# Early tiles of the busiest expert: their products issued in counted portions around the last chunk's routing, with weight splits, loads and output moved behind that chain

## The chip, the cores and the metric

One core of a Trainium2 chip runs the kernel. The metric is the device time of one execution in microseconds (us), the lower the better. TensorE is called PE here, VectorE DVE, ScalarE ACT, GpSimd POOL and the queue of SyncE SP, as in the profile.

## The reference

Three parts follow each other, all in float32.

```python
# 1: attention, 4 batches x 8 heads x 576 positions x 64: a local band plus a 4x downsampled one
x = (out_up + out_local)              # laid out as 2304 tokens x 512
# 2: a dense layer pair, 512 -> 2048 -> 512
h = np.maximum(x @ w_in, 0.0)
x = h * h @ w_out
# 3: eight experts, each token goes to one
logits = x @ w_gate                   # 2304 x 8
e_idx = np.argmax(logits, axis=1)
gate_w = softmax(logits)[token, e_idx]
eom = 1.0 / (1.0 + np.exp(-(x @ w_output_gate)))
for e in range(8):
    mask = e_idx == e
    ye = np.maximum(x[mask] @ w1[e], 0.0) @ w2[e]      # 512 -> 1024 -> 512
    out[mask] = gate_w[mask, None] * eom[mask, e, None] * ye
```

## The kernel before

**Stages.** Attention makes the 512 x 2304 activations in tiles of [128, 576]. Part 2 goes over nine chunks of 256 tokens: `l1` (products named `ph`) and `l2` (named `y`). Each float32 operand is split into a high and a low part, and each product is three passes (`PASSES`: high by high, high by low, low by high). When a chunk's `y` is done, `finish_y` copies it out of PSUM as `yr` (one half by ACT, one by DVE), and `routing` decides where its rows go.

**Routing of a chunk** is a generator with steps parted by `yield`. First it transposes `yr` (`yt`, L536) and copies the result out (`yT`). Then it makes logits (`lg`, L544), copies them (`lgt`) and sums their four parts (`lg` again, L550). DVE copies the sums (`lgs`, L553) and finds each row's expert. Then PE counts the rows of each expert ahead of each row (`rk`, L579), DVE makes the row's place (`di`, L588), and two indirect DMAs on POOL's queue put the token numbers into two lists in DRAM (`orders`, L594). The rows themselves go to a table in DRAM (`ytab`, L600).

**Part 3** takes one expert after the other in tiles of 128 rows. A tile's rows are gathered from `ytab` by the numbers in the lists, transposed (`px`), split (`xs`, high by ACT and low by DVE), multiplied by `w1` (`ph`, `layer1`), transposed again (`pt`, split into `hs`) and multiplied by `w2` (`py`, `layer2`). Weights come in eight loads of 128 x 1024 for each expert (0 to 3 are `w1`, 4 to 7 are `w2`); each is split by ACT (high) and DVE (low) out of a staging buffer. There are three such buffers at first, so load i waits for the DVE half of split i-3.

**The seam between parts 2 and 3.** No list is complete before the last chunk is routed. To have work for PE there, the kernel takes the expert with most rows so far (`choose`, "lead") and computes two of its tiles early, during the last chunk: `lead_1` makes `phf` (24 products a tile), `lead_turn` transposes (`ptf`) and splits (`hsf`), `lead_2` makes `pyf` (24 products) and puts the result out. `feed(n)` splits the first n of 16 weight pieces named in `LINE`. After the last routing, the heads of the lists are read back (`c4`, L943) and DVE makes the row numbers of the first two tiles of expert 0 (`cf`, `cd`, `ci`), which POOL gathers. The whole lists are read as `og` and transposed on PE (`po`, L986); DVE makes the index table of all later gathers from that.

**What sets the order.** The kernel is traced in program order, and a scheduler then orders each engine's instructions by its own simulated time. `high_priority` lets a block go first where it can; `issue_after(x)` queues a block's instructions behind x, but only those on the engine of x, and without waiting for x to finish. Each engine then runs its instructions strictly in that order.

```python
    route(1)
    lead_1(0, 0)
    feed(12)
    route(1)
    lead_1(0, 1)
    route(8)
```

Of the kernel before, what the change touches and what calls it, by code (L numbers as in the profile page):

```python
# [25 lines left out]
def attn_moe_kernel(  # L26
# [503 lines left out]
    def routing(c):  # L530
# [3 lines left out]
        for i in range(2):  # L534
            for kk in range(KC):
                nc.tensor.transpose(out=pt[:, i, P * kk:P * kk + P],  # L536
                                    in_=yr[:, i, P * kk:P * kk + P], identity=ident)
        yT = cv.tile([P, 2, DM], F32, tag="raw", name=f"yT{c}")
        nc.scalar.activation(out=yT[:, 0, :], in_=pt[:, 0, :], func=AF.Copy)
        nc.scalar.activation(out=yT[:, 1, :], in_=pt[:, 1, :], func=AF.Copy)  # L540
        yield
        pl = psa.tile([P, 2, DM], F32, tag="at", name=f"lg{c}")
        for kk in range(KC):
            nc.tensor.matmul(pl[32 * kk:32 * kk + 32, 1, 0:CH], lhsT=wg[:, kk, :],  # L544
                             rhs=yT[:, :, P * kk:P * kk + P], start=True, stop=True)
        lt = cv.tile([P, DM], F32, tag="tmp", name=f"lgt{c}", bufs=TMPB)[:, 0:CH]
        nc.scalar.activation(out=lt, in_=pl[:, 1, 0:CH], func=AF.Copy)
        plv = pl[:, 0, 0:4 * E].rearrange("p (i e) -> p i e", i=2)
        for i in range(2):
            nc.tensor.matmul(plv[:, i, :], lhsT=lt[:, P * i:P * i + P], rhs=psum4,  # L550
                             start=True, stop=True)
# [26 lines left out]
        for i in range(2):  # L578
            nc.tensor.matmul(prv[:, i, :], lhsT=sut, rhs=oh[:, i, :], start=True, stop=False)  # L579
            nc.tensor.matmul(prv[:, i, :], lhsT=ones, rhs=seen, start=False, stop=True)  # L580
# [12 lines left out]
        for i in range(2):  # L593
            nc.gpsimd.indirect_dma_start(  # L594
# [115 lines left out]
    def lead_split():  # L710
# [10 lines left out]
        most["hr"] = [late.tile([P, F2], F32, tag="hr", name="hr")] * 2  # L721

    def lead_1(x, h):

        ph = (psh.tile([P, DM], F32, tag="ph", name=f"phf{x}_{h}") if x == 0 else
              psy.tile([P, DM], F32, tag=f"y{h}", name=f"phf{x}_{h}"))
        half_layer1(ws[-1, 0], most["xs"][:, x], ph, most["hr"][x], h)

    def lead_turn(x):
# [3 lines left out]
        for h in range(2):  # L733
            t = psh.tile([P, DM], F32, tag="ph", name=f"ptf{x}_{h}")
            for c in range(4):
                f0 = 512 * h + P * c
                nc.tensor.transpose(out=t[:, P * c:P * c + P], in_=most["hr"][x][:, f0:f0 + P],
                                    identity=ident)
            nc.scalar.activation(out=hs[2 * h], in_=t, func=AF.Copy)
            nc.vector.tensor_sub(out=hs[2 * h + 1], in0=t, in1=hs[2 * h].bitcast(F32))  # L740
        most["hs", x] = hs

    def lead_2(x):
        py = psy.tile([P, DM], F32, tag=f"y{x}", name=f"pyf{x}")
        hs = most["hs", x]
        for kf in range(KF):
            for n, (a, b) in enumerate(PASSES):
                o = P * (kf % 4)
                nc.tensor.matmul(py, lhsT=hs[2 * (kf // 4) + a][:, o:o + P], rhs=ws[-1, 1](b, kf),
                                 start=(kf == 0 and n == 0), stop=(kf == KF - 1 and n == 2))  # L750
# [5 lines left out]
        nc.gpsimd.indirect_dma_start(  # L756
            out=out, out_offset=bass.IndirectOffsetOnAxis(ap=oi[:, 0:1], axis=0), in_=ob,
            in_offset=None, bounds_check=NT - 1, oob_is_err=False)
# [22 lines left out]
    def half_layer1(w1v, xs, ph, hr, h):  # L781
        for n in range(3 * KC):
            kk, (a, b) = n // 3, PASSES[n % 3]
            nc.tensor.matmul(ph, lhsT=xs[:, a, P * kk:P * kk + P],  # L784
                             rhs=w1v(b, kk)[:, 512 * h:512 * h + 512],
                             start=(n == 0), stop=(n == 3 * KC - 1))
        nc.scalar.activation(out=hr[:, 512 * h:512 * h + 512], in_=ph, func=AF.Relu)  # L787

    def layer1(w1v, xs, ph, hr):
        for h in range(2):  # L790
            half_layer1(w1v, xs, ph[h], hr, h)
# [139 lines left out]
    route(1)  # L931
    lead_1(0, 0)
    feed(12)
    route(1)
    lead_1(0, 1)
# [4 lines left out]
    with tc.high_priority():  # L940
        c4 = const.tile([P, 2, 2 * FT], F32, name="c4")
        for i, o in enumerate(orders):
            nc.sync.dma_start(out=c4[:, i, :], in_=lists(o)[0, :, 0:2 * FT])  # L943
# [252 lines left out]
```

## Time and profile before

| | |
|---|---|
| time, median of 3 runs | 917.65 us (916.43 to 921.03) |
| the profiled execution | 917.83 us |
| its span, first to last instruction | 916.0 us |
| PE busy | 823.5 us (90%) |
| DVE, ACT, POOL busy | 451.5, 395.9, 341.3 us |
| mean granted TensorE clock | 0.967 of full |
| DMA | 103.45 MB, mean 113 GB/s |

The span is what lies between the core's first and last instruction; the time holds 1.8 us around it. PE is busy almost everywhere; the page's 40 slices show two places where it is not, the start, and slices 28 and 29 of 40, which are the seam.

### The profile page before, as it was taken

The numbers are of one execution on the slowest core, as the hardware profiler recorded it, in microseconds if no ns is written. First come the engines' busy times: TensorE is split into PE (matmuls) and PEld (weight loads), VectorE is DVE, ScalarE is ACT, GpSimd is POOL, SyncE is SP. The second block draws the span as 40 slices with busy tenths as digits, with TensorE's granted clock in tenths as the row PEclk, the third lists the DMA queues.
The fourth block names the chain that finished last, engine by engine and source line by source line (L and its number), as shares of the span: only waits on it lengthen the run. The fifth ranks groups of instructions, "written<-read, shape, count | busy, mean of one in ns | idle before, by whom it ended". The sixth has DMA issues, their size and how long they took to land. (4 is left out here: it accounts for less than half of the span.)

```text
span 916.0 us, 15844 instructions
## 1 busy us (share of the span) xinstructions
PE 823.5 (90%) x5983; PEld 697.6 (76%) x5983; DVE 451.5 (49%) x960; ACT 395.9 (43%) x900; POOL 341.3 (37%) x411
## 2 busy tenths in 40 slices
PE   4588979987999989999999999993699989999996
PEld 3377869876888878888989898772587767878785
DVE  7987685777365554343222225425443556434111
ACT  3634555554443443343333335542544656434221
POOL 4556554544345543543333233313231232312111
PEclk9988989998899999999999999996799999999999
DMA  9851221454034332110000024415854594531101
GB/s 324 255 160 46 99 95 69 167 178 161 24 100 78 78 101 78 28 29 25 1 24 1 24 70 138 140 46 180 297 197 132 202 335 140 207 133 35 50 34 35
DMA packets 35519, 103.45 MB, mean 113 GB/s; under 512 B 6836, under 2 KB 6864, under 8 KB 35408
## 3 DMA queue, kind: packets, MB, share of 16 engines
q1 hardware_dynamic: 30000, 87.16, 28.9%
q0 software_dynamic: 5408, 14.88, 5.2%
q8 instruction: 61, 1.00, 0.5%
q14 instruction: 50, 0.41, 0.1%
HBM read 88.16 MB, written 14.65 MB: 112 GB/s over the span
## 5 line engine op out<-in xcount | busy, mean ns | idle before, releaser
L461 PE MATMUL ph<-xc,win 128*128 128x256 f32 x1728 | 244.1, 288 | 14.0 <-DVE g L466 12.1
L461 PEld LDWEIGHTS ph<-xc,win 128*128 128x128 f32 x1728 | 230.0, 193 | 33.1 <-DVE g L466 14.7
L484 PE MATMUL y<-wout,gs 128*128 128x512 f32 x864 | 231.8, 400 | 4.8 <-ACT gs L469 3.7
L470 POOL TENSOR_TENSOR gs<-g,gs 128x256 fp32r<-128x256 f32 x144 | 111.8, 779 | 201.6 <-ACT gs L469 129.7
L484 PEld LDWEIGHTS y<-wout,gs 128*128 128x128 f32 x864 | 151.7, 189 | 34.4 <-ACT gs L469 4.5
L466 DVE SCALAR_TENSOR_TENSOR g<-ph,g 128x256 f32<-128x256 f32 x144 | 60.2, 420 | 172.8 <-ACT g L465 172.6
L465 ACT ACTIVATE g<-ph 128x256 f32<-128x256 f32 x144 | 54.7, 382 | 122.6 <-PE ph L461 105.1
L469 ACT ACTIVATE gs<-g 128x256 fp32r<-128x256 f32 x144 | 59.6, 415 | 60.2 <-DVE g L466 54.8
L784 PE MATMUL ph<-we_wa,xs 128*128 128x512 f32 x228 | 64.5, 419 | 13.0 <-PEq L1127 8.4
L1024 POOL DMA_INDIRECT xg<-ytab,apt x23 | 32.2, 1400 | 84.4 <-ACT apt L787 44.4
L784 PEld LDWEIGHTS ph<-we_wa,xs 128*128 128x128 f32 x228 | 42.8, 197 | 24.9 <-ACT we_wd L650 8.8
L784 PE MATMUL ph<-we_wb,xs 128*128 128x512 f32 x228 | 61.4, 406 | 0.0
L1064 DVE COPY g<-g 128x2 f32<-128x2 f32 x19 | 3.2, 169 | 103.8 <-ACT ob L1055 103.8
L1051 PE MATMUL py<-we_wc,hs 128*128 128x512 f32 x216 | 54.1, 399 | 0.0
L1051 PE MATMUL py<-we_wd,hs 128*128 128x512 f32 x216 | 53.3, 396 | 0.0
L784 PEld LDWEIGHTS ph<-we_wb,xs 128*128 128x128 f32 x228 | 44.6, 196 | 11.1
L1055 ACT ACTIVATE ob<-py,g 128x512 f32<-128x512 f32 x18 | 12.4, 687 | 88.3 <-PE py L1051 78.5
L1058 POOL DMA_INDIRECT out_dram<-ob,oi x18 | 18.6, 1033 | 82.6 <-issue 34.6
L1051 PEld LDWEIGHTS py<-we_wd,hs 128*128 128x128 f32 x216 | 40.6, 188 | 9.8
L1051 PEld LDWEIGHTS py<-we_wc,hs 128*128 128x128 f32 x216 | 39.7, 188 | 8.7
L787 ACT ACTIVATE apt<-ph 128x512 f32<-128x512 f32 x38 | 22.8, 600 | 49.3 <-PE ph L784 49.2
L448 DVE TENSOR_TENSOR xc<-xT,xc 128x256 fp32r<-128x256 f32 (+3 forms) x76 | 37.3, 540 | 2.8 <-ACT xc L447 2.8
(257 smaller groups left out, 1223.3 us busy)
## 6 DMA issues: line engine op xcount, KB each, us to landing
apt<-in_w_dram SPq DMA_DIRECT2D x37, 512.0 KB, 4.1
stg<-in_w_dram SPq DMA_DIRECT2D x35, 512.0 KB, 7.2
apt<-in_qk_dram SPq DMA_DIRECT2D x10, 576.0 KB, 4.9
raw<-in_w_out_dram SPq DMA_DIRECT2D x11, 512.0 KB
raw<-in_w_in_dram SPq DMA_DIRECT2D x11, 512.0 KB, 3.3
ytab<-yr SPq DMA_DIRECT2D x18, 260.0 KB, 2.3
yr<-ypart SPq DMA_DIRECT2D x8, 512.0 KB, 4.3
sparewb<-in_qk_dram SPq DMA_DIRECT2D x6, 576.0 KB, 13.8
```

Source lines behind the costliest of these rows:

```text
L448: nc.vector.tensor_sub(out=t[:, 1, hp, done:done + ln], in0=src, in1=hi.bitcast(F32))
L461: nc.tensor.matmul(ph, lhsT=wv[:, wh, kk, :], rhs=x[:, xh, kk, :], start=(n == 0), stop=(n == 3 * KC - 1))
L465: nc.scalar.activation(out=g, in_=ph, func=AF.Relu)
L466: nc.vector.scalar_tensor_tensor(out=g, in0=ph, scalar=0.0, in1=g, op0=ALU.max, op1=ALU.mult)
L469: nc.scalar.activation(out=gs[:, 0, :], in_=g, func=AF.Copy)
L470: nc.gpsimd.tensor_sub(out=gs[:, 1, :], in0=g, in1=gs[:, 0, :].bitcast(F32))
L484: nc.tensor.matmul(yps[c][i], lhsT=gs[:, gh, P * i:P * i + P], rhs=woutv[f // FQ][:, f % FQ, wh, :], start=(first and n == 0), stop=(last ...
L784: nc.tensor.matmul(ph, lhsT=xs[:, a, P * kk:P * kk + P], rhs=w1v(b, kk)[:, 512 * h:512 * h + 512], start=(n == 0), stop=(n == 3 * KC - 1))
L787: nc.scalar.activation(out=hr[:, 512 * h:512 * h + 512], in_=ph, func=AF.Relu)
L1024: nc.gpsimd.indirect_dma_start(out=xg[:], out_offset=None, in_=ytab[:], in_offset=bass.IndirectOffsetOnAxis(ap=idx, axis=0))
L1051: nc.tensor.matmul(py, lhsT=hs[:, a, P * kf:P * kf + P], rhs=w2v(b, kf), start=(kf == 0 and n == 0), stop=(kf == KF - 1 and n == 2))
L1058: nc.gpsimd.indirect_dma_start(out=out, out_offset=bass.IndirectOffsetOnAxis(ap=oi[:, 0:1], axis=0), in_=ob[:], in_offset=None, bounds_che ...
```

## The change

The products of the early tiles become a generator that yields after each product (`lead_1` and `lead_turn` become parts of it). Of them, 10, 4 and 9 are issued behind the named steps of the last routing on PE (`yt`, first `lg`, second `lg`), 39 behind `rk`, and the rest later. The second `yT` copy of the last chunk goes to DVE. `feed` has split 14 pieces, not 12, before the routing, in another order of `LINE`; the two others stand behind `di` on DVE and behind `lgt` on ACT. The early tiles' output is put behind the list's puts on POOL, the loads of expert 1 behind the read of the list heads on SP, and the transposes of the lists behind the last early product on PE. At expert 0, the split of the second tile stands behind that of the first and behind its products, and so do the splits of expert 1's weights behind the first tile's split.

```diff
+        if c < NCH - 1:
+            nc.scalar.activation(out=yT[:, 1, :], in_=pt[:, 1, :], func=AF.Copy)
+        else:
+            nc.vector.tensor_copy(yT[:, 1, :], pt[:, 1, :])
...
-        nc.gpsimd.indirect_dma_start(
-            out=out, out_offset=bass.IndirectOffsetOnAxis(ap=oi[:, 0:1], axis=0), in_=ob,
-            in_offset=None, bounds_check=NT - 1, oob_is_err=False)
+        with tc.issue_after(most["put"].ins):
+            nc.gpsimd.indirect_dma_start(
+                out=out, out_offset=bass.IndirectOffsetOnAxis(ap=oi[:, 0:1], axis=0), in_=ob,
+                in_offset=None, bounds_check=NT - 1, oob_is_err=False)
...
-    LINE += [(lead, i) for i in range(4, 8)] + [(experts[0], i) for i in range(4, 8)]
+    LINE += [(x, i) for j in (4, 6) for x in (lead, experts[0]) for i in (j, j + 1)]
...
-    route(1)
-    lead_1(0, 0)
-    feed(12)
-    route(1)
-    lead_1(0, 1)
+    for _ in lead_1(0):
+        pass
+    feed(14)
+    fill = [lead_2(0), lead_2(1)]
+    for part, n in (("yt", 10), ("lg", 4), ("ps", 9)):
+        route(1)
+        with tc.issue_after(most[part]):
+            drive(fill, n)
     route(8)
...
-    lead_turn(0)
-    lead_1(1, 0)
-    lead_1(1, 1)
-    lead_2(0)
-    with tc.issue_after(most["routed"]):
+    with tc.issue_after(most["rk"]):
+        drive(fill, 39)
+    with tc.issue_after(most["routed"]), tc.issue_after(most["lt"]):
         feed(16)
...
-    lead_turn(1)
-    lead_2(1)
+    with tc.issue_after(most["rk"]):
+        drive(fill, 99)
...
-    with tc.issue_after(most["routed"]):
+    with tc.issue_after(most["routed"]), tc.issue_after(got.ins):
         for i in range(3):
             experts[1].load(i, stages[i])
...
+            with tc.issue_after(most["end"]):
+                nc.tensor.matmul(po[:, 0, h * E * NTL // 2:(h + 1) * E * NTL // 2],
...
+        with ExitStack() as behind:
+            if e == 0:
+                for x in (*first_xs, first_mm):
+                    behind.enter_context(tc.issue_after(x))
+            split_rows(xgs[1 + 2 * (e % 2)], xs1, g1, f"{e}_1")
```

The built order differs from that of before only from the last chunk's end to the first tile of expert 0. On PE, in the last chunk's routing, before: `yt` are the transposes of the chunk's result, `phf` and `ptf` the early tiles' products and transposes, `lg` the logits.

```order
L536 MATMUL yt_6514<-ident,yr_6505 128x128 x4
L784 MATMUL phf_0_6639<-we-1_wa,xsf 128x512 x6
L784 MATMUL phf_0_6639<-we-1_wb,xsf 128x512 x4
L536 MATMUL yt_6514<-ident,yr_6505 128x128 x4
L784 MATMUL phf_0_6639<-we-1_wb,xsf 128x512 x2
L784 MATMUL phf_1_6653<-we-1_wa,xsf 128x512 x3
L737 MATMUL ptf_1_6632<-ident,apt 128x128 x4
L784 MATMUL phf_1_6653<-we-1_wa,xsf 128x512 x3
L784 MATMUL phf_1_6653<-we-1_wb,xsf 128x512 x6
L544 MATMUL lg_6546<-yT_6523,wg 32x256 x4
```

The same place on PE in the change (its line numbers are 3 to 18 higher):

```order
L536 MATMUL yt_6553<-ident,yr_6505 128x128 x8
L745 MATMUL ptf_0_6569<-ident,apt 128x128 x4
L794 MATMUL phf_0_6583<-we-1_wa,xsf 128x512 x2
L745 MATMUL ptf_1_6576<-ident,apt 128x128 x4
L547 MATMUL lg_6586<-yT_6562,wg 32x256 x4
L794 MATMUL phf_0_6583<-we-1_wa,xsf 128x512 x4
L556 MATMUL lg_6586<-psum_82,lgt_6591 128x16 x2
L794 MATMUL phf_0_6583<-we-1_wb,xsf 128x512 x6
L794 MATMUL phf_1_6626<-we-1_wa,xsf 128x512 x3
L585 LDWEIGHTS sut
L585 MATMUL rk_6630<-oh_6609,sut 128x8
```

Before, 24 `phf` products and 4 `ptf` transposes stand between the first `yt` and the first `lg`, and 21 `pyf` products between the first and the second `lg`; now two products and four, and nine before `rk`.

On DVE, at the arithmetic on the list heads, before (`we` are low halves of weight splits, `cf`, `cd`, `ci` the row numbers of the first two tiles):

```order
L651 TENSOR_TENSOR we_wd<-apt,we_wd 128x1024
L651 TENSOR_TENSOR we_wa<-apt,we_wa 128x1024
L945 TENSOR_TENSOR cf<-c_6610 128x4
L947 TENSOR_TENSOR cd<-cf 128x2
L651 TENSOR_TENSOR we_wa<-apt,we_wa 128x1024
L949 SCALAR_TENSOR_TENSOR ci<-cd,star,cf 128x2
```

And in the change:

```order
L595 CAST di_6641<-rsc_6603 128x2
L658 TENSOR_TENSOR we_wd<-apt,we_wd 128x1024 x2
L963 TENSOR_TENSOR cf<-c_6651 128x4
L965 TENSOR_TENSOR cd<-cf 128x2
L967 SCALAR_TENSOR_TENSOR ci<-cd,star,cf 128x2
L672 COPY cntc<-pcc 128x8
L986 CAST nti<-cntc 128x8
L987 TENSOR_SCALAR nti<-nti 128x8
L749 TENSOR_TENSOR hsf_1_6704<-ptf_0_6707,hsf_0_6703 128x512
```

The splits of expert 1 (`we_wa`) are gone from between these rows, and the low part `hsf` of the second early tile, which stood ahead of `di` before, now stands behind `cf`.

On DVE, at the first tiles of expert 0, before (`g` is a copy of two columns of gathered rows, `g_6814` of those of the second tile; `xs_6812` is the first tile's low part):

```order
L1039 COPY g_139<-apt 128x2
L1064 COPY g_6816<-g_139 128x2
L1039 COPY g_6814<-apt 128x2
L1040 TENSOR_TENSOR xs_6812<-px_0_6818,xs_6812 128x512
L1040 TENSOR_TENSOR xs_6806<-px_1_6885,xs_6806 128x512
L651 TENSOR_TENSOR we_wb<-stg_6813,we_wb 128x1024
```

And in the change, where the second `g_139` is that of expert 1's first tile:

```order
L1057 TENSOR_TENSOR xs_6812<-px_0_6818,xs_6812 128x512
L1056 COPY g_6814<-apt 128x2
L658 TENSOR_TENSOR we_wa<-apt,we_wa 128x1024
L1056 COPY g_139<-apt 128x2
L658 TENSOR_TENSOR we_wa<-apt,we_wa 128x1024
L658 TENSOR_TENSOR we_wb<-apt,we_wb 128x1024
L658 TENSOR_TENSOR we_wb<-stg_6813,we_wb 128x1024
L1057 TENSOR_TENSOR xs_6806<-px_1_6885,xs_6806 128x512
```

The first tile's low part no longer stands behind the copy from the second tile's rows; three of expert 1's split halves now stand behind the copy from a gather of expert 1.

## Rows read from the trace of the kernel before

**Rows 1.** Windows of 5 us: length, busy time (instructions) of PE, PEld, DVE, ACT, POOL, clock, DMA share, GB/s.

```profile
625.00:630.00 5.00, 0.00 (x0) 0.00 (x0) 1.23 (x1) 1.12 (x2) 1.51 (x3) 0.65 0.23 30
```

**Rows 2.** Waits after 660 us: who waited for whom, us in all, times, longest.

```profile
PE ph L784 <- PEq L1127: 8.4, 2, 4.4
```

**Rows 3.** Timeline of the last routing: start, length, engine, line, output<-inputs, [idle before <-releaser].

```profile
600.76 0.69 DVE L523 COPY yr<-y 128x512 f32<-128x512 f32 x1 [3.36 <-PE y L484]
...
604.93 0.60 PE L536 MATMUL yt<-ident,yr 128*128 128x128 f32 x4
...
606.06 0.59 ACT L540 ACTIVATE yT<-yt 128x512 f32<-128x512 f32 x1
...
609.17 0.64 PE L544 MATMUL lg<-yT,wg 128*32 128x256 f32 x8
...
612.65 2.26 PE L749 MATMUL pyf<-we-1_wd,hsf 128*128 128x512 f32 x9
614.75 0.51 PE L550 MATMUL lg<-psum,lgt 128*128 128x16 f32 x4
...
615.37 0.19 DVE L553 COPY lgs<-lg 128x32 f32<-128x32 f32 x1 [6.87 <-PE lg L550]
...
619.37 0.16 DVE L588 CAST di<-rsc 128x2 int32<-128x2 f32 x1
```

**Rows 4.** Timeline: list puts and read-backs, of the routing before (570s) and the last.

```profile
571.15 1.07 POOL L594 DMA_INDIRECT order<-row,di  x1 [0.72 <-PE ph L461]
...
575.71 1.95 SPq L699 DMA_DIRECT2D of<-order  x2
...
579.42 0.16 DVE L702 TENSOR_TENSOR oif<-of 128x2 int32<-128x2 f32 x1 [1.30 <-DMA of<-order]
...
619.81 1.69 POOL L594 DMA_INDIRECT order<-row,di  x1 [1.63 <-DVE di L588]
621.81 2.10 POOL L594 DMA_INDIRECT order<-row,di  x1 [0.30 <-issue]
628.80 0.55 POOL L965 DMA_DIRECT2D og<-order  x1 [0.58 <-DMA order<-row,di]
629.29 0.46 SPq L943 DMA_DIRECT2D c<-order  x1
635.82 0.16 DVE L945 TENSOR_TENSOR cf<-c 128x4 f32<-128x4 f32 x1
```

**Rows 5.** Timeline from the last early products to expert 1's first product.

```profile
619.44 1.22 DVE L651 TENSOR_TENSOR we_wc<-apt,we_wc 128x1024 fp32r<-128x1024 f32 x1
...
621.13 2.97 PE L749 MATMUL pyf<-we-1_wd,hsf 128*128 128x512 f32 x12
...
637.54 0.30 DVE L996 CAST apt<-po 128x144 int32<-128x144 f32 x1
...
640.05 0.23 DVE L1002 TENSOR_TENSOR apt<-po,sh 128x64 int32<-128x64 f32 x1
...
645.61 0.17 DVE L1039 COPY g<-apt 128x2 f32<-128x2 f32 x1 [4.00 <-DMA apt<-ytab,ci]
...
646.40 3.76 PE L784 MATMUL ph<-we_wa,xs 128*128 128x512 f32 x8
...
653.86 0.60 PE L1069 MATMUL pt<-ident,apt 128*128 128x128 f32 x4
...
660.19 2.15 PE L784 MATMUL ph<-we_wa,xs 128*128 128x512 f32 x5 [4.38 <-PEq L1127]
```

**Rows 6.** Windows of 0.5 us of PE: length, busy time (instructions), clock, DMA share, GB/s.

```profile
626.00:626.50 0.50, 0.00 (x0) 0.95 0.00 0
...
660.50:661.00 0.50, 0.50 (x3) 0.59 0.87 107
...
663.50:664.00 0.50, 0.50 (x3) 0.50 1.01 352
```

**Rows 7.** DMA issues of 600 to 665 us: queue, count, KB each, median us to landing.

```profile
apt<-ytab,apt POOLq DMA_INDIRECT x3, 6.7
```

More of the change, by code (lines that the diff above doesn't have):

```diff
@@ L579, in routing @@
             nc.tensor.matmul(prv[:, i, :], lhsT=sut, rhs=oh[:, i, :], start=True, stop=False)
-            nc.tensor.matmul(prv[:, i, :], lhsT=ones, rhs=seen, start=False, stop=True)
+            most["rk"] = nc.tensor.matmul(prv[:, i, :], lhsT=ones, rhs=seen, start=False,
+                                          stop=True).ins
             nc.vector.tensor_add(out=seen, in0=seen, in1=oh[:, i, :])
@@ L593, in routing @@
         for i in range(2):
-            nc.gpsimd.indirect_dma_start(
+            most["put"] = nc.gpsimd.indirect_dma_start(
                 out=orders[i][:], out_offset=bass.IndirectOffsetOnAxis(ap=di[:, i:i + 1], axis=0),
@@ L720, in lead_split, with lead_1, lead_2 @@
         most["xs"] = xs
[L721 to L729, printed above, removed]
+        most["hr"] = late.tile([P, F2], F32, tag="hr", name="hr")
+    def lead_1(x):
+        for h in range(2):
+            ph = (psh.tile([P, DM], F32, tag="ph", name=f"phf{x}_{h}") if x == 0 else
+                  psy.tile([P, DM], F32, tag=f"y{h}", name=f"phf{x}_{h}"))
+            yield from half_layer1(ws[-1, 0], most["xs"][:, x], ph, most["hr"], h)
+    def lead_2(x):
         hs = [xp.tile([P, S], F32, tag="xT", name=f"hsf{x}_{i}").bitcast(F32R)[:, 0:512]
@@ L736, in lead_turn @@
                 f0 = 512 * h + P * c
-                nc.tensor.transpose(out=t[:, P * c:P * c + P], in_=most["hr"][x][:, f0:f0 + P],
+                nc.tensor.transpose(out=t[:, P * c:P * c + P], in_=most["hr"][:, f0:f0 + P],
                                     identity=ident)
+                yield
             nc.scalar.activation(out=hs[2 * h], in_=t, func=AF.Copy)
             nc.vector.tensor_sub(out=hs[2 * h + 1], in0=t, in1=hs[2 * h].bitcast(F32))
-        most["hs", x] = hs
-    def lead_2(x):
+        if x == 0:
+            yield from lead_1(1)
         py = psy.tile([P, DM], F32, tag=f"y{x}", name=f"pyf{x}")
-        hs = most["hs", x]
         for kf in range(KF):
@@ L748, in lead_2 @@
                 o = P * (kf % 4)
-                nc.tensor.matmul(py, lhsT=hs[2 * (kf // 4) + a][:, o:o + P], rhs=ws[-1, 1](b, kf),
-                                 start=(kf == 0 and n == 0), stop=(kf == KF - 1 and n == 2))
+                most["end"] = nc.tensor.matmul(
+                    py, lhsT=hs[2 * (kf // 4) + a][:, o:o + P], rhs=ws[-1, 1](b, kf),
+                    start=(kf == 0 and n == 0), stop=(kf == KF - 1 and n == 2)).ins
+                yield
         ob = most["xe"][:, x, 0:DM]
@@ L942, in attn_moe_kernel @@
         for i, o in enumerate(orders):
-            nc.sync.dma_start(out=c4[:, i, :], in_=lists(o)[0, :, 0:2 * FT])
+            got = nc.sync.dma_start(out=c4[:, i, :], in_=lists(o)[0, :, 0:2 * FT])
         cf = const.tile([P, 2 * FT], F32, name="cf")
@@ L1018, in attn_moe_kernel @@
     early[3] = mp2.tile([P, 1024], F32, tag="stg3", name="stg3", bufs=1)
-    hr = most["hr"][0]
+    hr = most["hr"]
     g1, gn, gp = (mp2.tile([P, 2], F32, tag=f"g{i}", name=f"g{i}", bufs=1) for i in range(3))
@@ L1039, in split_rows @@
             nc.vector.tensor_copy(g, xg[:, DM:DM + 2])
-        nc.vector.tensor_sub(out=xs[:, 1, :], in0=px, in1=xs[:, 0, :].bitcast(F32))
+        lo = nc.vector.tensor_sub(out=xs[:, 1, :], in0=px, in1=xs[:, 0, :].bitcast(F32))
+        return hi.ins, lo.ins
     def layer1_here(w1v, xs, name):
-        layer1(w1v, xs, [ps4.tile([P, 512], F32, tag="ph", name=f"ph{name}_{h}")
+        return layer1(w1v, xs, [ps4.tile([P, 512], F32, tag="ph", name=f"ph{name}_{h}")
                          for h in range(2)], hr)
@@ L1097, in attn_moe_kernel @@
             after.place(0)
-            for i in range(4):
-                after.split(i)
+            with ExitStack() as behind:
+                if e == 0:
+                    for x in first_xs:
+                        behind.enter_context(tc.issue_after(x))
+                for i in range(4):
+                    after.split(i)
             for i in range(4, 8):
@@ L1105, in attn_moe_kernel @@
             after.place(1)
-        split_rows(xgs[1 + 2 * (e % 2)], xs1, g1, f"{e}_1")
+        with ExitStack() as behind:
+            if e == 0:
+                for x in (*first_xs, first_mm):
+                    behind.enter_context(tc.issue_after(x))
+            split_rows(xgs[1 + 2 * (e % 2)], xs1, g1, f"{e}_1")
         gather(xgs[2], index(e, 2))
@@ L1109, in attn_moe_kernel @@
             gather(xgs[3 - 2 * (e % 2)], index(e + 1, 1))
-        hand_over(g0, n)
+        turned = hand_over(g0, n)
         if more:
-            split_rows(xgs[0], xs0, g0, f"{e + 1}_0")
+            with tc.issue_after(turned):
+                split_rows(xgs[0], xs0, g0, f"{e + 1}_0")
             if e + 2 < E:
```

46 lines of the change are left out of this document (26 added, 20 removed).

## The prediction

> **What bounds the kernel now.** I read first the windows of 5 us over the page's weak slices, then the timeline of each engine there, then the waits of what follows. The windows show where PE has nothing to do: from 625 to 630 us it is not busy at all and its granted clock falls [rows 1]. The timeline gives the edges: the last early product ends at 624.1 (621.13 + 2.97), and the first product of expert 0 starts at 646.40 [rows 5]. Between them lie only the transposes of the lists and of two tiles of rows: 22.3 us in which PE waits for one chain, and that chain began before 600 us.
>
> The chain is the last routing. The chunk's result is out of PSUM at 601.45 (600.76 + 0.69), its first logits start at 609.17, the second at 614.75, DVE copies them at 615.37 and has the places at 619.37 [rows 3]. Up to the logits' copy that is 13.9 us for little work: the second half of the transposes starts only at 604.93, the first logits stand behind the second tile's products, and the second logits behind 21 products, of which nine are the row from 612.65 to 614.75 [rows 3]. These nine also give the pitch used below: 2.10 / 9 = 0.233 us a product. Then come two list puts, whose landing frees the read-backs at about 628.8 and 629.29, DVE's `cf` at 635.82 [rows 4], and the rows' gathers. At the end the first tile's low part stands on DVE behind a copy that waits for the second tile's gather until 645.61 [rows 5].
>
> What follows the seam takes a gain on: after 660 us PE's largest wait is the branch at L1127, twice, 8.4 us together, 4.4 at most [rows 2]. From expert 1's first product at 660.19 [rows 5] on, PE is the bound, and it has the same work in the same order. So I work out when that product comes. Everything ahead of 600 us keeps its order but for the load order, treated at the end of the next part.
>
> **The change, step by step.** Times are those of the profiled execution, 917.83 us with a span of 916.0, 0.18 above the median of the runs shown.
>
> *Routing on PE and ACT.* One more early product stands ahead of the chunk's last six: the result is out at 601.45 + 0.23 = 601.7. Eight transposes at the pitch of the row (four in 0.60 with their drain [rows 3]) end at 602.8. ACT has a relu copy of the same size ahead and copies its half (0.59 [rows 3]) until 603.45; in the built program DVE's half waits for ACT's, so moving it gains nothing: 0.69 like the copy of the result, to 604.2. The first logits start at 604.25 instead of 609.17. They take 0.64, their copy (half the columns of the 0.59, estimated 0.4) ends at 605.35; the four early products behind them (0.93) hold PE until 605.65, so the second logits start there, and DVE's copy 0.62 later (615.37 - 614.75) at 606.3, 9.1 us earlier than now.
>
> *To the places.* Before, 4.0 us from that copy to `di` (619.37 - 615.37), with two `hsf` parts of some 0.69 in between that now come later. Against that, ACT does two weight halves ahead of the exponentials that DVE waits for, and nine products (2.1) stand ahead of `rk`. Bounds 2.6 and 4.0; by the list of instructions I get 3.9, nearer the upper: `di` at 610.2.
>
> *Puts and read-back.* The first put starts 0.44 after `di` (619.81 - 619.37), the second 2.0 later as in the last routing, where DVE's split halves of 1.22 ran beside it [rows 4, 5], and where they run again: 612.6. If it were as short as in the routing before (1.07 + 0.30), 612.0. From the second put's start to its landing took 7.0 (621.81 to 628.80), with weight loads beside it; in the routing before, a first put took 4.6 (571.15 to 575.71) [rows 4]. The weight loads are now in earlier. So the second read-back is issued between 616.6 and 619.7. It then takes 0.46 to issue and 1.76 to land (577.66, the end of the issue, to 579.42 [rows 4]): the list heads are in SBUF between 618.8 and 621.9. I take the middle, 620.3. No row shows more than an upper end for that read beside weight loads: `cf` ran 6.5 us after its issue, at 635.82, behind a split half [rows 4]. That is the bound on the late side, 626.1.
>
> *The new wait.* DVE now runs `cf` ahead of the second tile's low part `hsf`, so DVE sits from about 612.6 until the heads land. Behind it stand six small operations (0.16 each and the gap, 0.2) and that `hsf` (0.69): it ends at 622.3. PE has by then run nine products to 610.9, 24 to 616.5, eight transposes to 617.5, waited 0.6 for ACT's part, and done two products to 618.6. The third needs `hsf`: PE stalls 3.7 us. That is part of the old stall, come back in the middle of the fill. 22 products are left, 5.1 us: 627.4.
>
> *The clock.* After the last early product PE idled 2.3 us before the clock fell at about 626.45; after the idle of 4.38 it fell at 660.6, once work had begun again, and stood at half until 664.0 [rows 5, 6]. The new stall of 3.7, almost all idle, lies between. I take the fall, as after the 4.38: 3.4 us at half speed cost 1.7, so the products end at 629.1. The Trainium skill speaks against the change in the same sense: TensorE: Matmul & The Clock Gate, section "HAM oscillation — how this bites in real kernels", has waits for data in the midst of matmuls lead to a restart at the lower clock. By it the sum is the one below; were the stall too short for it, 1.7 less.
>
> *First tile of expert 0.* The transposes of the lists, estimated as twice the row of four at 653.86 (0.60 [rows 5]), end at 630.3. DVE's arithmetic took 637.54 to 640.28 with one split half in between: 1.5 without it [rows 5], so 632.0 with semaphores. The low part follows at once (0.69 and a copy): 632.8. By then PE has done the rows' transposes and the four products that need only the high part. The other 20 end at 637.5. The gather of the rows (POOL, from 621) and the transposes' input (the list reads, from about 617) are hidden under the fill. Moving `xs` away from the second gather removes the wait that ended at 645.61 [rows 5].
>
> *To expert 1.* From the end of these products to the branch's end took 6.3 (653.86 to 660.19 [rows 5]); that gives 643.8. DVE gives another date: expert 1's first gather goes out when the arithmetic is done, 632.1, and takes 6.7 [rows 7]: 638.8. Behind its copy DVE now has three split halves (3 x 1.22) and four parts of 0.69, 6.5 in all: 645.3; two products can start ahead of the last: 644.8. The two dates lie close; I take 644.6. Against 660.19 that is 15.6 us. Arithmetic queued behind `po`, the early output behind the puts on POOL, and loads of expert 1 behind the read of the heads on SP cost nothing here: PE is filling, and the loads have from 620 to 630. Without that cover the output put would cost its own 1 us of POOL ahead of the gather.
>
> *Load order.* `LINE` now loads two pieces of expert 0 ahead of two of the lead. ACT's last square of the chunk stands behind the lead's fourth such piece. Its buffer is freed by a DVE half that now stands ahead of the chunk's last two squares on DVE, where before it stood behind them, so I price it at nothing; if the load held ACT, the whole chain would start later by as much.
>
> **Sum:** 917.83 - 15.6 = 902.2, or 902 for the median.
>
> **The rivals.**
>
> *Late reads and gathers.* The heads land between 622 and 626.1, or the gather of expert 1 takes over 7 us under the five loads issued beside it, or the load order holds ACT: each us beyond the estimate costs one. With the heads at 626.1: 902.2 + 5.8 = 908. For it: the old read-backs and gathers all ran beside loads. Against: the earlier loads are done.
>
> *No stall in the fill.* If the heads land before about 616.6, `hsf` is there when PE wants it; neither 3.7 nor 1.7 is paid: 896.8. Against it: a put took 4.6 at least [rows 4], and this asks for 4 from the first put's start to both read-backs in. The Trainium skill's page DMA: Bandwidth & Descriptors, "Anatomy of one DMA — SWDGE (gpsimd) path", puts a transfer at about 2 us plus its bytes; by that estimate the heads would be in at about 616.7, and the sum near 897. The rows have over twice that for the put.
>
> *The gain is absorbed.* Expert 1's last five loads still go out only after the index table's register reads, and its weights are now wanted 16 us sooner; if they were the bound, the date of 660.19 would shift by a few us only: 913 to 918. Against it: DMA had nothing for most of 625 to 630 (share 0.23) [rows 1], and PE showed no such wait after 660.
>
> *Slower.* DVE's in-order wait for the heads now holds the fill. Over 0.5% slower would need the heads after 620.3 + 15.6 + 4.6 = 640.5, 21 us after the latest issue of their read; that read was in within 6.5.
>
> **How the numbers follow.** 0.5% of the time, 4.6 us, is about what a measurement of this kernel can tell from no change. Chances: the forecast (899 to 906) 0.55; late reads 0.27; no stall 0.08; absorbed 0.06; slower 0.04. Its early end has the heads at 618.8 (1.5 less) and no fall of the clock (1.7 less): 899.0; its late end the heads at 621.9 and the gather late by 2. The range reaches over the late reads and toward the case without a stall: 897 to 909, leaving out the other three, below 0.2. Faster are the first three, 0.90; same 0.06; slower 0.04.
>
> **What the changed profile would show.** `lgs` at about 606.3 and `di` at about 610; the second read-back of the heads issued near 618 and `cf` near 620; PE waiting for `hsf` for 3 to 4 us in the second tile's `pyf`, with the clock at half for some us after it; the first `ph` product near 631.5; the branch's 4.4 us unchanged, ending near 644.6; then no new wait of PE to the end. I would be wrong if PE waits for weights of expert 1 or 2 after that, if the logits still start after 607, or if the first product of expert 0 waits for rows and not for the fill.

## The result, and the profile after

The changed kernel takes 904.88 us (median of 4 runs, 903.22 to 906.1) against 918.22 for the kernel before beside it: ratio 0.9851, 95% interval 0.9819 to 0.9883. A second group of five runs gave 905.36 against 918.85, 0.9853 (0.9835 to 0.9871). That is 13.3 to 13.5 us less, 1.5%. The forecast was 902, its range 897 to 909.

| | before | after |
|---|---|---|
| profiled execution, its span | 917.83, 916.0 us | 903.22, 901.4 us |
| PE busy | 823.5 us (90%) | 821.4 us (91%) |
| mean granted clock | 0.967 | 0.973 |

First the last routing and the lists in the timeline of after, where [rows 3, 4] stand before:

```profile
598.42 0.69 DVE L523 COPY yr<-y 128x512 f32<-128x512 f32 x1 [4.53 <-PE y L484]
...
601.60 0.64 PE L547 MATMUL lg<-yT,wg 128*32 128x256 f32 x8
...
603.21 0.51 PE L556 MATMUL lg<-psum,lgt 128*128 128x16 f32 x4
...
603.83 0.19 DVE L559 COPY lgs<-lg 128x32 f32<-128x32 f32 x1 [0.95 <-PE lg L556]
...
607.12 0.17 DVE L595 CAST di<-rsc 128x2 int32<-128x2 f32 x1
607.20 2.35 DVE L658 TENSOR_TENSOR we_wd<-apt,we_wd 128x1024 fp32r<-128x1024 f32 x2
607.57 1.83 POOL L601 DMA_INDIRECT order<-row,di  x1 [13.09 <-DVE di L595]
...
609.71 0.98 POOL L601 DMA_INDIRECT order<-row,di  x1 [0.30 <-issue]
...
617.14 0.55 POOL L981 DMA_DIRECT2D og<-order  x1 [3.66 <-DMA order<-row,di]
618.92 0.16 DVE L963 TENSOR_TENSOR cf<-c 128x4 f32<-128x4 f32 x1 [9.37 <-DMA c<-order]
```

From the start of the result's copy `yr` to `di` it is now 8.7 us (607.12 - 598.42) where it was 18.6 (619.37 - 600.76 [rows 3]): the first logits no longer wait behind products, and the second only behind the four put there. But DVE stands idle for 9.37 ahead of `cf`. What that does to PE, in its timeline from there to expert 1's first product, for [rows 5] of before:

```profile
615.46 0.73 PE L756 MATMUL pyf<-we-1_wc,hsf 128*128 128x512 f32 x2 [0.33 <-ACT hsf L748]
620.67 4.28 PE L756 MATMUL pyf<-we-1_wc,hsf 128*128 128x512 f32 x10 [4.48 <-DVE hsf L749]
624.79 2.96 PE L756 MATMUL pyf<-we-1_wd,hsf 128*128 128x512 f32 x12
627.58 1.01 PE L1003 MATMUL po<-ident,og 72*128 72x72 f32 x8
...
629.72 1.19 PE L794 MATMUL ph<-we_wa,xs 128*128 128x512 f32 x4 [0.69 <-ACT xs L1054]
...
635.86 0.60 PE L1052 MATMUL px<-ident,apt 128*128 128x128 f32 x4
636.30 1.13 PE L1087 MATMUL pt<-ident,apt 128*128 128x128 f32 x8
637.52 0.63 PE L1052 MATMUL px<-ident,apt 128*128 128x128 f32 x4
644.66 2.90 PE L794 MATMUL ph<-we_wa,xs 128*128 128x512 f32 x6 [6.52 <-PEq L1155]
```

The 22.3 us without products are gone: the second tile's products, which had run before the wait, now lie in it. Three idle stretches are left: 4.48 for `hsf`, small ones for `xs`, and 6.52 ahead of expert 1, where the branch (L1155, before L1127) stands; `PEq` is PE's sequencer, which takes it. PE's granted clock in windows of 0.5 us (length, PE busy (instructions), clock, DMA share, GB/s; 1.00 is 2.4 GHz, 0.50 is 1.2 GHz), for [rows 6]:

```profile
617.00:617.50 0.50, 0.00 (x0) 1.00 0.00 0
617.50:618.00 0.50, 0.00 (x0) 0.57 0.18 2
...
624.00:624.50 0.50, 0.50 (x3) 0.60 0.93 305
624.50:625.00 0.50, 0.50 (x3) 1.00 0.73 255
641.00:641.50 0.50, 0.00 (x0) 0.97 1.18 412
641.50:642.00 0.50, 0.00 (x0) 0.50 0.90 347
...
648.00:648.50 0.50, 0.50 (x3) 0.71 0.80 320
```

The clock falls in both idle stretches and comes back 3.6 to 3.7 us after work resumed. Of PE's waits after 643 us, one differs by more than 0.6 us from those of before, the branch [rows 2]:

```profile
PE ph L794 <- PEq L1155: 10.7, 2, 6.5
```

**How executions are compared.** The start of that `yr` copy wanders from one execution to the next, whatever the order of the work: 598.42, 600.00, 600.52, 601.33 and 602.81 in five kernels that are alike up to there. So all that follows counts from it. By that measure expert 1's first product moved from 59.4 us (660.19 - 600.76) to 46.2, and to 46.7 and 46.0 in two further profiles (e5 and e6 below): 12.7 to 13.4 us, close to the gain in the medians. The kernel before has one profile only. What follows that product changed little: 255.8 us before (916.0 - 660.19), 256.7 after (901.4 - 644.66).

### The profile page after: what moved, and what is told of

It reads as the page before. It is cut to its first block, busy times and chain, and to the rows that moved or that the text cites. A ratio compares the mean times of both kernels' runs of the same rounds, so it can differ in the third digit from the quotient of the medians.

```text
span 901.4 us, 15844 instructions
## 1 busy us (share of the span) xinstructions
PE 821.4 (91%) x5983; PEld 695.4 (77%) x5983; DVE 450.6 (50%) x961; ACT 395.3 (44%) x899; POOL 341.6 (38%) x411
## 3 DMA queue, kind: packets, MB, share of 16 engines
q1 hardware_dynamic: 30000, 87.16, 28.9%
## 5 line engine op out<-in xcount | busy, mean ns | idle before, releaser
L1041 POOL DMA_INDIRECT xg<-ytab,apt x23 | 33.2, 1442 | 88.2 <-ACT apt L799 44.4
L794 PEld LDWEIGHTS ph<-we_wb,xs 128*128 128x128 f32 x228 | 43.6, 191 | 11.7 <-issue 1.1
L1076 POOL DMA_INDIRECT out_dram<-ob,oi x18 | 18.6, 1034 | 82.6 <-issue 36.2
## 6 DMA issues: line engine op xcount, KB each, us to landing
sparewb<-in_qk_dram SPq DMA_DIRECT2D x6, 576.0 KB, 13.1
```

Of the source, the lines that this page charges most:

```text
L794: mm = nc.tensor.matmul(ph, lhsT=xs[:, a, P * kk:P * kk + P], rhs=w1v(b, kk)[:, 512 * h:512 * h + 512], start=(n == 0), stop=(n == 3 * KC ...
L1041: nc.gpsimd.indirect_dma_start(out=xg[:], out_offset=None, in_=ytab[:], in_offset=bass.IndirectOffsetOnAxis(ap=idx, axis=0))
L1076: nc.gpsimd.indirect_dma_start(out=out, out_offset=bass.IndirectOffsetOnAxis(ap=oi[:, 0:1], axis=0), in_=ob[:], in_offset=None, bounds_che ...
```

## The experiments

A first entry is the changed kernel itself, run again as an anchor:

> The changed kernel itself once more, as the anchor for the other three of this group. All theories: 904 to 906 us; the branch before expert 1's products 6.1 to 6.6 us if its length follows the order of the work and not chance.

It did as expected on all counts. Distances in us from the start of `yr`, each read in that kernel's timeline; "branch" is the length of PE's branch ahead of expert 1's products, and "expert 1" is the first of these products.

| kernel | ratio to before (95%) | `di` | `cf` | first `ph` | branch | expert 1 |
|---|---|---|---|---|---|---|
| before | 1 | 18.6 | 35.1 | 45.6 | 4.56 | 59.4 |
| changed | 0.9851 (0.9819 to 0.9883) | 8.7 | 20.5 | 31.3 | 6.36 | 46.2 |
| e5, changed again | 0.9853 (0.9835 to 0.9871) | 8.7 | 20.0 | 31.1 | 6.58 | 46.7 |
| e6, edit without effect | 0.9844 (0.9827 to 0.9862) | 8.7 | 20.2 | 31.2 | 6.84 | 46.0 |
| e1, products not in portions | 0.9996 (0.9976 to 1.0016) | 23.4 | 35.3 | 44.8 | 6.52 | 61.0 |
| e8, portions alone | 0.9912 (0.9897 to 0.9927) | 9.1 | 25.0 | 35.7 | 6.18 | 50.1 |
| e9, all but portions | 0.9948 (0.9931 to 0.9964) | 18.4 | 31.5 | 40.2 | 6.10 | 56.0 |
| e2, old load order | 0.9875 (0.9851 to 0.9898) | 9.3 | 22.0 | 33.7 | 6.12 | 48.1 |
| e3, old order of expert 0 | 0.9875 (0.9851 to 0.9899) | 8.7 | 20.2 | 34.6 | 7.20 | 50.1 |
| e4, heads behind `hsf` | 0.9828 (0.9805 to 0.985) | 8.7 | 21.4 | 28.9 | 6.52 | 44.6 |
| e7, and lists late | 0.9853 (0.9834 to 0.9873) | 8.7 | 18.8 | 29.9 | 6.16 | 46.9 |
| e10, expert 1's loads held | 0.9889 (0.9861 to 0.9917) | 8.7 | 21.1 | 32.8 | 3.41 | 50.1 |
| e11, expert 2's loads held | 0.983 (0.9809 to 0.9852) | 8.7 | 20.9 | 32.3 | 5.68 | 45.9 |
| e12, e4, e11 and one more | 0.9828 (0.9802 to 0.9853) | 8.7 | 21.2 | 30.5 | 4.58 | 44.4 |

### Which part carries the gain

My theory was that the gain is the routing chain, moved ahead of the products by the portions; the rival, that expert 0's order or the loads carry it. **e1** takes the portions away:

```diff
     for part, n in (("yt", 10), ("lg", 4), ("ps", 9)):
         route(1)
-        with tc.issue_after(most[part]):
-            drive(fill, n)
+        drive(fill, n)
...
-    with tc.issue_after(most["rk"]):
-        drive(fill, 39)
+    drive(fill, 39)
...
-    with tc.issue_after(most["rk"]):
-        drive(fill, 99)
+    drive(fill, 99)
```

> The changed kernel, but its early tiles' products stand on PE as before (no portions behind the routing's steps); loads, output, list transposes and expert 0's order stay as changed. My theory: the gain is the routing chain, result out to destinations in 8.0 us where it was 17.9. Undone, di, both puts and the heads come about 9.9 us later, and the first tile's rows land at about 636 where they landed at 626; the stall of 4.5 us in the early tiles is gone, since DVE's hsf then stands ahead of cf. First expert product some 8 us later than in the changed kernel: 911 to 915 us. Rival: most of the gain comes from the other parts (expert 0's order, load order), and the portions give 3 us or less: 905 to 908 us.

It took 919.03 us: no gain is left, more than I expected. The expectation was wrong in one thing: "as before" is not what this edit makes. PE's timeline:

```profile
609.38 0.64 PE L547 MATMUL lg<-yT,wg 128*32 128x256 f32 x8
...
613.95 0.52 PE L556 MATMUL lg<-psum,lgt 128*128 128x16 f32 x4
...
620.66 0.18 PE L585 MATMUL rk<-oh,sut 128*128 128x8 bf16 x1
```

The rank products `rk` stand 6.7 us behind the second logits here, behind all 24 products of the second tile, where the kernel before had even `di`, which comes after `rk`, 4.6 behind them (619.37 - 614.75 [rows 3]). The chain to `di` is 23.4 us long, against 18.6. The branch is 2.0 us longer as well, and expert 1 starts 1.6 later than before although the first `ph` is 0.8 earlier. So e1 shows that the other parts give nothing behind so late a chain, but not how the gain divides. **e8** and **e9** do. e8 keeps the portions and the move of the `yT` copy, which no run parts from them, and takes all else back; e9 is the kernel before with all else added. The core of that rest, as it stands between e8 and the changed kernel:

```diff
-    LINE += [(lead, i) for i in range(4, 8)] + [(experts[0], i) for i in range(4, 8)]
+    LINE += [(x, i) for j in (4, 6) for x in (lead, experts[0]) for i in (j, j + 1)]
...
-    feed(12)
+    feed(14)
...
-            for i in range(4):
-                after.split(i)
+            with ExitStack() as behind:
+                if e == 0:
+                    for x in first_xs:
+                        behind.enter_context(tc.issue_after(x))
+                for i in range(4):
+                    after.split(i)
```

> Only the counted portions of the early tiles' products and the routing's own edits are kept; load order, the fences of output, lists and expert 1's loads, and expert 0's order are as in the kernel before. My theory: the portions carry most of the gain, and the other parts cost what they cost alone, about 2 us each: 908 to 911 us. Rival: the other parts give nothing by themselves when they are all undone together (906 us or less), or the portions need them, and most of the gain is gone (914 us or more).

> The kernel before with everything of the change but the portions: load order and feeds, the fences of the output, of the list transposes and of expert 1's loads, and expert 0's order; the early tiles' products stand on PE as in the kernel before, so result out to di takes about 17.9 us. Measured so far: all of the change 0.985, portions alone 0.991, all but the portions in the changed kernel's code 1.000. Theory A (the parts add): the rest gives the difference of 0.991 and 0.985, some 5 us: 913 to 914.5 us. Theory B (the rest is worth something only once the routing chain is early): 916.5 to 919 us.

e8 gave 910.29, 0.9912; e9 gave 916.16, 0.9948, beside a kernel before that took 920.25 in its group, so the ratio is what counts. The parts add: 0.9912 x 0.9948 = 0.986, against 0.9852 for the whole, and theory B of e9 (0.998 and up) lies outside its interval. So the portions bring some 8 us, the rest some 5; by expert 1's first product in the table they bring 9.4 and 3.4. In e9 `di` comes as late as before (18.4), but `cf` follows 13.1 behind it and not 16.5, and the first `ph` 8.8 behind `cf` and not 10.6.

### The load order

**e2** puts the loads back (the first two edits of the diff above, reversed, and one fence of `feed(16)`).

> The changed kernel with the order and the fences of the lead's and expert 0's loads and weight splits as before (12 steps fed instead of 14, the last ones behind the routing alone). My theory, as in the prediction: load order is worth nothing to 1 us: 904.5 to 906.0 us. Rival: the earlier splits are what lets the first products of the early tiles begin earlier, and this gives 2 us or more: 907 us and up.

907.06 us, ratio 0.9875: 2.1 us more than the changed kernel by the ratios, the intervals overlapping. Expert 1's first product came 1.4 to 2.1 later (table). The upper end of my expectation was 906.0, and the rival's range began at 907; but its reason is not what the profile shows: the early products begin 7.5 us ahead of `yr`, in the changed kernel 7.7. The profile has another mechanism. DVE's timeline in e2:

```profile
608.83 2.36 DVE L658 TENSOR_TENSOR we_wc<-apt,we_wc 128x1024 fp32r<-128x1024 f32 x2
611.10 1.22 DVE L658 TENSOR_TENSOR we_wd<-apt,we_wd 128x1024 fp32r<-128x1024 f32 x1
```

And POOL's beside it:

```profile
609.21 1.83 POOL L601 DMA_INDIRECT order<-row,di  x1 [12.51 <-DVE di L595]
611.34 1.83 POOL L601 DMA_INDIRECT order<-row,di  x1 [0.30 <-issue]
```

Two more weight pieces are left for DVE to split here, and its halves run beside both puts; each takes 1.83. In the changed kernel they end at 609.55 (607.20 + 2.35), and the second put takes 0.98 (both rows in the first fence above). With `di` 0.6 later that gives `cf` 1.5 to 2.0 later, and the early tiles' stall is 5.39 instead of 4.48.

### Expert 0's order

**e3** takes back the fences of expert 0's splits (the last edit in the diff above, reversed), those of the second tile's `xs` and the one of expert 1's first rows.

> The changed kernel with expert 0's order as before: the second tile's transposes and copies, and expert 1's weight splits, are not held behind the first tile's xs. My theory: xs of the first tile stands again behind work that waits for the second tile's rows, some 1.2 to 3 us on PE's first expert product: 906 to 908 us. Rival (expert 0's order carries the gain): 910 us or more. Second rival: it carries nothing, 904 to 905.5 us.

908.45 us, ratio 0.9875, 2.1 us more than the changed kernel by the ratios with overlapping intervals, and 3.4 to 4.1 by expert 1's first product: the price I expected or somewhat more, for another reason. ACT's timeline in e3:

```profile
623.47 1.06 ACT L657 ACTIVATE we_wa<-apt 128x1024 fp32r<-128x1024 f32 x1 [11.42 <-DMA apt<-in_w_dram]
...
625.00 0.59 ACT L748 ACTIVATE hsf<-ptf 128x512 fp32r<-128x512 f32 x1
```

And PE's:

```profile
625.64 5.39 PE L756 MATMUL pyf<-we-1_wc,hsf 128*128 128x512 f32 x12 [7.74 <-ACT hsf L748]
```

Not the second tile's rows: a split of expert 1's weights now stands on ACT ahead of `hsf` and waits 11.42 us for its load. PE's stall in the fill is 7.74. In e8 the same split waits 7.97 us for its load in the same place. So, by these profiles, the work of the fence on the splits is to keep a wait for weights out of ACT's queue while the early tiles need it.

### The stall for the list heads

**e4** moves `cf`, `cd`, `ci` and the row gathers in DVE's and POOL's order behind the last `hsf`:

```diff
+            most["low"] = nc.vector.tensor_sub(out=hs[2 * h + 1], in0=t, in1=hs[2 * h].bitcast(F32)).ins
...
     with tc.issue_after(most["rk"]):
         drive(fill, 99)
+    with tc.high_priority(), tc.issue_after(most["low"]):
+        cf = const.tile([P, 2 * FT], F32, name="cf")
...
```

> The changed kernel with DVE's cf, cd, ci and the row gathers queued behind the last hsf of the second early tile; PE's order is the same. My theory: PE's stall of 4.48 us before its x10 group and the half clock behind it (about 1.9 us) go, the early tiles end near 622 instead of 628.4, and the next bound is the row gather's landing (near 626): the first expert product comes 1.5 to 2.5 us earlier, 902 to 903.5 us. Rival A: the stall is fully on the path, all 6.4 us come back, 898 to 899 us. Rival B: the stall was cover for the gather, nothing comes back, or cf comes later than before: 904 to 907 us.

903.93 us, ratio 0.9828: 2.1 us less than the changed kernel by the ratios, 1.0 by the medians, the intervals overlapping. Expert 1's first product came 1.4 to 2.1 earlier (table). That is my theory's size. The time excludes rival A (6.4 back); against rival B (nothing back) speak only the profiles. PE's timeline shows where the stall went:

```profile
618.50 3.32 PE L756 MATMUL pyf<-we-1_wc,hsf 128*128 128x512 f32 x12 [0.33 <-ACT hsf L748]
621.66 2.96 PE L756 MATMUL pyf<-we-1_wd,hsf 128*128 128x512 f32 x12
624.47 1.01 PE L1004 MATMUL po<-ident,og 72*128 72x72 f32 x8
628.59 1.09 PE L1053 MATMUL px<-ident,apt 128*128 128x128 f32 x4 [3.12 <-DMA apt<-ytab,ci]
630.37 3.78 PE L794 MATMUL ph<-we_wa,xs 128*128 128x512 f32 x8 [0.69 <-ACT xs L1055]
```

The fill no longer stops; PE waits behind it for the rows, 3.12 us, and the half clock goes along (8 products in 3.78; the granted clock is 0.50 in the windows from 628 to 633.5; before the change they ran at the same pace, 3.76 [rows 5]). Only the difference comes back.

**e7** asks what holds the second put's landing. In the changed kernel it starts at 609.71 and has landed when POOL's second read `og` goes at 617.14. Here, on top of e4, both reads of the whole lists go behind the row gathers:

```diff
+    with tc.issue_after(rows.ins):
+        ogs = []
+        for o in orders:
...
```

> As the kernel with DVE's cf behind the last hsf (903.9 us), and besides the two reads of the whole lists (og) issued on POOL behind the row gathers. Theory A: these reads, with packets of 4 bytes, are what kept the second put from landing (5.5 us behind its packets): cf then comes 9 to 10 us behind di instead of 12.7, rows and first products 2 to 3 us earlier; the list arithmetic waits for the later reads, near 629, which takes some of it back: 901.5 to 904 us. Theory B: the second put lands as late without them (12 to 13 us from di to cf), and the later lists cost 1 to 3 us: 904.5 to 907 us.

`cf` came 10.1 us behind `di`, against 11.4 to 12.7 in e4, e5, e6 and the changed kernel: these reads cost the heads 1.3 us or more. The time is 904.41, the border of the two theories, and nothing is gained on e4: DVE's list arithmetic, which now waits for the lists until 629.93, stands ahead of the first tile's `xs` (631.64). Most of the put's landing stays unexplained.

### The branch

The branch took 4.56 us before and 6.1 to 7.2 in the changed kernel and e1 to e9. In the kernel before, the DMA was idle in part of it (share 0.46 over the branch, 0.00 in two windows of 0.5 us), in the others it was not (0.96 to 1.03). **e6** was to hold loads back behind `xs`, by a fence on a DVE instruction:

> The changed kernel with the loads of expert 1's second layer (stages 4 to 7) issued behind the xs of its first tile (about 643) and no longer from 633 on, so that little is on the DMA while PE takes the branch. Theory A: the branch takes longer when the DMA is busy (4.56 us in the kernel before, 6.36 in the changed one): it falls to 4.5 to 5 us; PE then waits for xs (643.5), and its first product of expert 1 comes about 1 us earlier; the second layer's weights come 5 to 10 us later, which may cost as much: 903.5 to 907 us. Theory B: the length of the branch has nothing to do with these loads: 6 to 6.6 us as before, and the time is the same or longer.

It tested nothing. The fence orders instructions of one engine, and SP issued the loads from 629.0 on as ever; e6 is one more run of the changed kernel. **e10** makes SP itself wait, by a read of `xs`:

```diff
-            for i in range(4, 8):
-                after.load(i, stages[i])
+            if e:
+                for i in range(4, 8):
+                    after.load(i, stages[i])
...
+            if e == 0:
+                q = mp2.tile([1, 2], F32, tag="q", name="q", bufs=1)
+                held = nc.sync.dma_start(out=q, in_=xs0[0:1, 1, 0:2].bitcast(F32))
+                with tc.issue_after(held.ins):
+                    for i in range(4, 8):
+                        after.load(i, stages[i])
```

> The changed kernel with expert 1's second layer loads (stages 4 to 7) held on SP behind a read of 8 bytes of its first tile's xs, so that SP issues none of them between 627 and about 646. Theory A: PE's branch before expert 1's products takes longer when its instruction fetch meets the weight loads: with the DMA nearly idle it takes 4.5 to 5 us where it took 6.2 to 6.8 in all kernels with loads in flight; the later weights may cost more than that: 904 to 912 us. Theory B: the length of the branch is not set by the loads: 6 us or more again.

The branch's row in e10 (count, shortest/median/longest in ns, first and last start):

```profile
L1162 PEldq COMPARE_BRANCH  x1: 3406/3406/3406, 641.1 to 641.1; - x1
```

The window of its length there (busy time (instructions) of PE, PEld, DVE, ACT, POOL, then clock, DMA share, GB/s):

```profile
641.10:644.50 3.40, 0.34 (x4) 0.10 (x1) 2.52 (x5) 1.15 (x3) 1.89 (x2) 1.00 0.45 105
```

The branch's row in the changed kernel:

```profile
L1155 PEldq COMPARE_BRANCH  x1: 6359/6359/6359, 638.1 to 638.1; - x1
```

And the window of its length:

```profile
638.10:644.50 6.40, 0.04 (x1) 0.00 (x0) 6.40 (x8) 4.68 (x6) 1.20 (x1) 0.76 1.00 371
```

3.41 us with the DMA moving 105 GB/s, 6.36 with 371: theory A, beyond its number. The kernel as a whole lost, 910.59, since PE then waited 9.14 us, put down to ACT's first split of the held weights (649.48 + 1.06 = 650.54; PE went on at 650.58). **e11** holds not expert 1's loads but expert 2's, which nobody needs yet, by the same read of `xs` ahead of them, behind SP's own branch. **e12** is e4 and e11 together, with DVE's copy of expert 1's gate columns behind its `xs`:

```diff
-            for i in range(4):
-                experts[e + 2].load(i, stages[i])
+            with ExitStack() as behind:
+                if e == 0:
+                    q = mp2.tile([1, 2], F32, tag="q", name="q", bufs=1)
+                    held = nc.sync.dma_start(out=q, in_=xs0[0:1, 1, 0:2].bitcast(F32))
+                    behind.enter_context(tc.issue_after(held.ins))
+                for i in range(4):
+                    experts[e + 2].load(i, stages[i])
```

> The changed kernel with expert 2's first loads (which SP issued from 633 on, during PE's branch) held on SP behind a read of 8 bytes of expert 1's xs, near 645; expert 1's own loads stay where they are. Theory A (the branch is lengthened by loads in flight): the branch takes 3.4 to 5 us instead of 6.2 to 6.8, and PE's next bound is xs, which ends 1.0 us ahead of the branch in the changed kernel's profile: 903.5 to 905 us, against 905.1 for the changed kernel. If the later prefetch is late for its splits, that is given back: 905 to 907 us. Theory B: the branch stays at 6 us or more, and the time stays.

> Three edits on the changed kernel: cf and the row gathers behind the last hsf (0.983 of before by itself), expert 2's first loads held behind expert 1's xs, and DVE's copy of expert 1's gate columns put behind its xs so that the weight splits no longer wait for that gather. Theory A: branch 3.4 to 5 us, xs some 1.5 us earlier: the first product of expert 1 comes 1.5 to 2.5 us earlier than with the first edit alone, 901 to 903 us. Theory B (nothing on the branch to be had, or what is gained is lost behind it): 903.5 to 905 us.

The branch took 5.68 us in e11 (DMA share 0.73), more than theory A's 3.4 to 5, and 4.58 in e12 (0.40). The times, 905.98 and 905.45 beside a kernel before of 921.81 in that group, are 0.983 and 0.9828. Against the changed kernel's 0.9852 that is some 2 us, within the intervals; and e12 is no faster than e4, whose stall edit it contains; the 1.5 to 2.5 us of its theory A did not come (44.4 against 44.6 in the table). Its branch is 1.9 us shorter than e4's, but its rows landed 7.4 us behind `cf` (630.93 - 623.54) and not 5.7, and that took most of it back. So by their ratios e4, e11 and e12 lie some 2 us ahead of the changed kernel, and no run separates them. For e11 the profile doesn't bear it out: its first product of expert 1 stands at 45.9, where e6 has it at 46.0.

## Why the prediction was right, and where its sum was off

The forecast held: the mechanism named (routing ahead of the products, a new wait on DVE, the clock's fall behind it, expert 1's first product as the date that counts) is what the profile shows. The sum was 2.2 to 2.9 us too good: a shift of 15.6 against 12.7 to 13.4. Counted from the end of the result's copy (601.7 in the prediction, 599.11 and 600.69 in two profiles of the changed kernel; work on PE ends where its next begins):

| step | predicted | profile | second |
|---|---|---|---|
| `lgs` starts | 4.6 | 4.7 | 4.7 |
| `di` starts | 8.5 | 8.0 | 8.0 |
| second put starts | 10.9 | 10.6 | 10.6 |
| heads in, `cf` | 18.6 | 19.8 | 19.4 |
| PE's stall for `hsf`, length | 3.7 | 4.48 | 4.05 |
| early products end | 27.4 | 28.5 | 28.3 |
| the 20 `ph` end | 35.8 | 36.8 | 36.5 |
| expert 1's first product | 42.9 | 45.6 | 46.0 |

- **Routing and places:** right within 0.5 us. DVE's half of `yT` did wait for ACT's (1.74 idle), so the move gained nothing.
- **Puts and read-back:** too short by 1.1 to 1.5 us from the second put to `cf` (7.7 in the prediction, 9.2 and 8.8 measured). The middle between the bounds was taken; the put landed 7.4 us after its start (609.71 to 617.14), later than the 7.0 taken as the upper end, although the weight loads were done (5 GB/s on average from 610 to 615). e7 gives the list reads 1.3 us of it; the rest is open.
- **New wait and clock:** both there. The ten products behind the stall took 4.12 us (624.79 - 620.67) and at the full pitch would take 2.33: 1.8, against 1.7. The Trainium skill's rule (TensorE: Matmul & The Clock Gate, "HAM oscillation — how this bites in real kernels") that a wait for data amid matmuls lowers the clock held here: it fell 1.4 us into the idle (616.19 to 617.57, by the window's mean of 0.57).
- **First tile of expert 0:** from the early products' end to the end of the 20 `ph` 8.4 us were predicted and 8.3 measured. But moving `xs` off the second gather was not all that the new order does: e3 shows that it keeps ACT's queue free for `hsf`, which the prediction did not see.
- **To expert 1:** this is the term that was furthest off. The sum has 7.1 us here (637.5 to 644.6), between PE's old 6.3 and DVE's date, with "the branch's 4.4 us unchanged". It was 8.8 us (644.66 - 635.86): one more row of four transposes ahead, and the branch 1.8 longer, now that it lies among the loads. The shift alone is not what put it there: in e1 and e9, where PE reaches it only 0.4 and 5.0 us earlier than before, counted from `yr` (15.1 in the changed kernel), it takes 6.52 and 6.10 as well. The second date, DVE's, was 0.8 late (its last `xs` ends at 43.6 in the prediction and at 44.4, 643.47, in the profile), and had the branch been short, `xs` would have been the bound, 1.0 us ahead of the branch's end (644.46).
- **Load order, priced at nothing:** e2 measures 2.1 us, with overlapping intervals. By the profiles the price lies at the puts, where the prediction had the row for it (a put of 2.10 beside a split half [rows 4]) but expected the halves to run there again.
- **Rivals:** late reads came in part (the heads 0.8 to 1.2 late), within the forecast's own range. No stall: e4 shows why its 5.4 us were never there; with the stall gone, PE waits for the rows. Absorbed and slower did not come.

## What to carry to other kernels

Where a kernel has one serial chain (here routing, lists, gathers) and a pool of independent products, count the products into the chain's gaps and queue nothing else ahead of the chain, on any engine: e3 lost some 2 us by one split on ACT, e2 as much by two pieces on DVE. When a stall is named, say what waits next before pricing its removal: of 6.4 us only some 2 came back in e4. And when a branch lies on the path, look at what the DMA moves while it is taken; a date behind a branch doesn't carry over when the transfers around it move.

## What was not expected of the hardware

PE's branch to code it then runs lasted 3.41 us with the DMA at a share of 0.45 over it (0.00 for most of its first microsecond), 4.56 and 4.58 at 0.46 and 0.40, 5.68 at 0.73 and 6.1 to 7.2 at 0.96 to 1.03. The share alone does not set the length (3.41 and 4.56 go with nearly the same share). In the kernel before and the changed one, a second branch at the same line, some 85 us later, took 5.78 us at a share of 0.82 and 5.94 at 0.89. The profile's instruction queues have three or four packets there; that these are what the loads delay is a guess, and only the lengths are shown.

A put of 128 list places occupied POOL for 0.97 to 0.98 us alone and 1.82 to 1.83 beside DVE's halves of 128x1024, in the changed kernel, e2, e3 and e8; in the kernel before, 1.69 and 2.10 beside them [rows 4, 5]. The Trainium skill (DMA: Bandwidth & Descriptors, "SWDGE vs HWDGE vs iDMA") has DVE lock GpSimd out of the memory in which it writes descriptors while it runs in its two-port mode; that these halves, which read two inputs, run in that mode no run here shows, and the reason stays open.
